# Pair sums one pair ahead, two buffers for their float32 weights, and GpSimd's last instruction

## Chip, core and metric

The kernel runs on one core of one Trainium2 chip. The metric is device time in microseconds (us) of one execution, as the median of several runs. Engines are called as the profile calls them: PE (TensorE matmul), PEld (its weight loads), DVE (VectorE), ACT (ScalarE), POOL (GpSimd), SP (SyncE, which only issues DMA transfers here, strictly in order).

## What is computed

Three stages in a row: causal attention mixed with a linear memory, and two gated feed-forward layers over the same 2304 tokens (4 sequences of 576, width 512 = 8 heads of 64, hidden width 1536).

```python
a = softmax(causal(q @ k.T / 8)); local = a @ v                       # per head, S = 576
mem = (phi(q) @ M_prev) / (phi(q) @ z_prev + 1e-6)                    # phi(x) = max(x, 0) + min(exp(x), 1)
x = sigmoid(beta) * mem + (1 - sigmoid(beta)) * local                 # -> 2304 x 512
xn = x / rms(x) * rms_g
x = (silu(xn @ w_gate) * (xn @ w_val)) @ w_out                        # layer 0
out = (sigmoid(x @ w2_gate) * (x @ w2_val)) @ w2_out                  # layer 1
```

## The kernel before

The tokens go through in five groups: first the first 128 tokens of all four sequences together (`g = -1`, 512 tokens, their attention written out by hand in the string `ORDER`), then the other 448 tokens of each sequence (`g = 0` to `3`). While PE does the two feed-forward layers of group g, the attention of group g+1 is traced in between, one step of the list `att_steps` after so many slices; `total` sets the pace (`len(steps) * (done - wait) // (total - wait)`). A scheduler then orders each engine's instructions, so program order is only partly the order of tracing.

A layer's hidden width is cut into 12 slices of 128 (`f`). A slice is two products with K = 512 (`pg`, gate, and `pv`, value, line 807), the nonlinearity on ACT and DVE (`gated`), and the slice's share of the layer's output (`out_share`, line 863, 12 matmuls into four accumulators `po`). Weights and tokens are split into two float16 or float32r parts, so each product is three matmuls.

In the last group (`last_slices`, `g = 3`) some slices go in pairs (`UNITS`: pairs 0-1 to 8-9 in layer 0, 3-4 to 9-10 in layer 1). `hidden_pair` computes a pair's 2 x 2 block product with seven products instead of eight (Winograd's form of Strassen's scheme; matmuls on line 959, results in `pw`). It needs sums of the two slices' weights: `weight_sums` loads the float32 weights of both slices (`kept`, two DMAs, line 912, tile `rw`), adds them on DVE (lines 919 and 927, tile `sw`), and splits the result into two float16 parts on ACT (929) and DVE (930). The products' partial sums are copied by ACT (`keep_sum`, 977) and added by DVE into `cw` (lines 980 and 1004). PE may write an accumulator again only after that DVE add has read it.

`rw` is the one buffer with tag "x" (before that, the attention's input). Of all pairs, only the first of layer 0 loads into spare weight slots. Weights themselves live in a ring of 13 slots (`ws`, `wl`, `wr`, `wrl`); a slot's load is issued by SP once its last reader is through.

POOL does four kinds of work. At the start it makes an identity and a causal mask (memsets, then AFFINE_SELECT, `masks.py:199` and line 92) from which ACT casts `ident_b` and `tri_b`, the operands of PE's first score matmuls (line 261). Up to 54 us it does some elementwise work of the first group (350, 343, 383). From then on it does only maxima over the partitions (PARTITION_ALL_REDUCE), the last of them for the scale of layer 1's tokens (`xtop`, line 1022). The built program has an instruction without operands, printed as ISA, ahead of POOL's first AFFINE_SELECT and another ahead of its first all-reduce.

After `xtop`, DVE multiplies the per-slice scales `unit[2]` of layer 1 by the new token scale (line 1167, ten slices at once).

```python
def unit_slices(f):
    nc.vector.tensor_scalar(
        out=unit[2][:, f], in0=unit[1][:, f], scalar1=st["half_is1"], scalar2=None, op0=ALU.mult
    )
```

Of the kernel before, what the change touches and what calls it, by code (L numbers as in the profile page):

```python
# [33 lines left out]
NWIDE = 2  # L34
# [26 lines left out]
def attn_moe_moe_kernel(ctx, tc, qT, kT, qk0, v, mz, beta, w8, rms_g, outT):  # L61
# [840 lines left out]
            nc.vector.tensor_scalar(out=q[:, 3], in0=q[:, 3], scalar1=half_isx, scalar2=None, op0=ALU.mult)  # L902
        return q

    def weight_sums(l, f, q, spare=False):

        raw = [slot(B - 1, F32) for i in range(2)] if spare else None
        if not spare:
            two = ap_.tile([128, 5, DM], F32, tag="x", name="rw")
            raw = [two[:, 2 * i:2 * i + 2] for i in range(2)]  # L910
        for i in range(2):
            nc.sync.dma_start(out=raw[i], in_=kept[l, f + i])
        out = []
        for m in range(2):
            part = lambda i, j: raw[i][:, m, 256 * j:256 * j + 256]
            ratio, less, scale = (q[:, c, (f - PAIRED[l]) // 2, m:m + 1] for c in (1, 2, 3))
            sw = ap_.tile([128, SW], F32, tag="sc", bufs=2, name="sw")[:, 0:1024]
            a = sw.rearrange("p (j n) -> j p n", j=4)
            nc.vector.tensor_tensor(out=a[0], in0=part(1, 0), in1=part(1, 1), op=ALU.add)
            for j, (x, c, y, op) in enumerate(  # L920
                (
                    (part(0, 0), less, a[0], ALU.add),
                    (part(0, 0), ratio, part(1, 0), ALU.subtract),
                    (part(0, 1), ratio, a[1], ALU.subtract),
                )
            ):
                nc.vector.scalar_tensor_tensor(out=a[j + 1], in0=x, scalar=c, in1=y, op0=ALU.mult, op1=op)  # L927
            w = slot(B - 1, F16).rearrange("p a b n -> p a (b n)")
            nc.scalar.activation(out=w[:, 0], in_=sw, func=AF.Copy, scale=scale)
            nc.vector.scalar_tensor_tensor(  # L930
                out=w[:, 1], in0=sw, scalar=scale, in1=w[:, 0], op0=ALU.mult, op1=ALU.subtract
            )
            out.append(w)
        return out

    def hidden_pair(ws, sums, l, f, xh, xs, hs, outs):

        n = NT
        regions = []
        for pool, tag in (("mm", "mm"), ("ps", "pa")):  # L940
            two = [late[pool].tile([128, 512], F32, tag=tag, name="pw") for _ in range(2)]
            regions.append([two[i // 2][:, 256 * (i % 2):256 * (i % 2) + n] for i in range(4)])

        def left(i, m, a, k):
            if i >= 3:
                return sums[m][:, a, 256 * (i - 3) + 128 * k:256 * (i - 3) + 128 * k + 128]
            c = 128 * k + (256 if i else 0)
            return ws[1 if i == 2 else 0][m][:, a, c:c + 128]

        def right(i, b, k):  # L950
            if i >= 3:
                return xs[b][:, i - 3, k]
            return xh[b][:, k + (2 if i else 0), n if i == 2 else 0:2 * n if i == 2 else n]

        def product(m, at, i, j, first=False):
            c = 0
            for k in range(2):
                for a, b in ((0, 0), (0, 1), (1, 0)):
                    nc.tensor.matmul(  # L959
                        regions[m][at],  # L960
                        left(i, m, a, k),
                        right(j, b, k),
                        start=first and c == 0,
                        stop=c == 5,
                        skip_group_check=True,
                    )
                    c += 1

        cs = []
        for m, tag in ((0, "kk"), (1, "qq")):  # L970
            cs.append([ap_.tile([128, S], F32, tag=tag, bufs=2, name="cw")[:, 0:2 * n] for _ in range(2)])
        one = [ap_.tile([128, S], F32, tag=t, bufs=1, name="sn") for t in ("kd", "qd")]
        three = [ap_.tile([128, 512], F32, tag=t, bufs=1, name="sn") for t in ("mx", "mb")]
        snaps = [[one[m][:, 0:n], one[m][:, n:2 * n], three[m][:, 0:n]] for m in range(2)]

        def keep_sum(m, i):
            nc.scalar.copy(out=snaps[m][i], in_=regions[m][0])

        def add(m, i, j, at, s):
            nc.vector.tensor_tensor(out=cs[m][i][:, j * n:(j + 1) * n], in0=regions[m][at], in1=snaps[m][s], op=ALU.add)  # L980

        R, Y, Q, V = range(4)
        A11, A12, A22, S1, S2, S3, S4 = range(7)
        B11, B21, B22, T1, T2, T3, T4 = range(7)
        for m in range(2):
            product(m, R, A11, B11, True)
            keep_sum(m, 0)
        for m in range(2):
            product(m, Q, A12, B21, True)
            add(m, 0, 0, Q, 0)  # L990
        for m in range(2):
            product(m, R, S2, T2)
            keep_sum(m, 1)
        for m in range(2):
            product(m, V, S1, T1)
        outs[0]()
        for m in range(2):
            product(m, R, S3, T3)
            keep_sum(m, 2)
            add(m, 1, 1, V, 2)  # L1000
        outs[1]()
        for m in range(2):
            product(m, Y, A22, T4)
            nc.vector.tensor_tensor(out=cs[m][1][:, 0:n], in0=snaps[m][2], in1=regions[m][Y], op=ALU.subtract)
        gated(cs[0][1], cs[1][1], l, f + 1, 2 * n, B - 1, hs[1])
        for m in range(2):
            product(m, V, S4, B22)
            add(m, 0, 1, V, 1)
        gated(cs[0][0], cs[1][0], l, f, 2 * n, B - 1, hs[0])
# [135 lines left out]
    def last_of(e):  # L1145
        return next(i for i in reversed(nc.cur_bb.bb.instructions) if i.engine == e)
# [14 lines left out]

    def first_sums(l):
        q = firsts["q", l] = pair_units(l)
        firsts[l] = weight_sums(l, PAIRED[l], q, l == 0)

    def unit_slices(f):
        nc.vector.tensor_scalar(
            out=unit[2][:, f], in0=unit[1][:, f], scalar1=st["half_is1"], scalar2=None, op0=ALU.mult
        )

    def last_slices(l, n, xt, halves, xs, po):
        g, f, pending, done = B - 1, 0, [], [0]
        ws, hs = {}, {}

        def share(i):
            out_share(ws[i], hs[i], po, n, done[0] == 0, done[0] == NF - 1)
            done[0] += 1

        for k, size in enumerate(UNITS[l]):
            for i in range(f, f + size):  # L1180
                ws[i] = weights(g, l, i)
                hs[i] = htiles(g, l, i)
            if l == 1 and f == NWIDE:
                unit_slices(slice(NWIDE, NF))
            if size == 2:
                sums = firsts[l] if f == PAIRED[l] else weight_sums(l, f, firsts["q", l])
                shares = [lambda: None] * (2 - len(pending)) + [lambda i=i: share(i) for i in pending]
                hidden_pair([ws[f], ws[f + 1]], sums, l, f, halves, xs, [hs[f], hs[f + 1]], shares)
                pending = [f + 1, f]
            else:  # L1190
                hidden(ws[f], l, f, n, g, halves if is_half(g, l, f) else xt, hs[f])
                for i in pending:
                    share(i)
                pending = [f]
            f += size
            if l == 0 and f == NF - 2:
                first_sums(1)
        for i in pending:
            share(i)

    for g in range(-1, B):
        n = 512 if g < 0 else S - 128
        steps = list(att_steps(g + 1)) if g + 1 < B else []

        total = 2 * NF - (8 if g <= 0 else 4 if g == 1 else 7)

        wait = 2 if g == 0 else 1
        if g == 0:
# [2 lines left out]
        for l in range(2):  # L1211
# [10 lines left out]
            for f in range(0 if g == B - 1 else NF + 1):  # L1222
                if f < NF:
                    if f >= early:
                        if g > 0 and l == 1 and f == NWIDE:
                            unit_slices(slice(NWIDE, NF))
                        turn = lagged(4 if g < 0 else 3) if g <= 0 else []
                        if g >= 0 and l == 0 and f in (1, 2):
                            turn = turn + tokens_done
                        with behind(turn):  # L1230
                            ws.append(weights(g, l, f))
                        hs.append(htiles(g, l, f))
                        if g == B - 2 and l == 1 and f == NF - 2:
                            first_sums(0)
                        hidden(ws[f], l, f, n, g, xh if l == 1 and is_half(g, l, f) else xt, hs[f])
                        marks.append(tuple(last_of(e) for e in (mybir.EngineType.Activation, mybir.EngineType.DVE)))
# [87 lines left out]
```

## Time and profile before

| what | before |
|---|---|
| time, median of 3 runs | 1061.79 us (1058.84 to 1062.64) |
| the profiled execution: its time, its span | 1061.79 us, 1060.0 us |
| PE busy | 1026.0 us (97% of the span), 6801 matmuls |
| DVE, ACT, POOL busy | 814.6, 591.8, 91.2 us |
[...]
| chain that ended last | PE 74%, DVE 11%, "issue" 6%, DMA 5%, ACT 3%, POOL 1% |

The span runs from the first to the last instruction of the execution; 1.8 us lie around it. "Issue" is time in which an engine waited for nothing that the profile shows. Busy time of PE is partly modelled, so only its gaps are read here, not its speed.

### The profile page before, as it was taken

What the parts mean: (1) busy time and instruction counts of PE and PEld (TensorE: products, weight loads), DVE (VectorE), ACT (ScalarE), POOL (GpSimd) and SP (SyncE); (2) the same over time, 40 slices, a digit from 0 to 9 for tenths busy, and PEclk for the clock granted to TensorE, in tenths of its full rate; (3) what the DMA queues carried; (4) which work ended last, traced back from release to release, by engine and by line L of the source; (5) the groups of instructions that cost most, each with busy time, mean ns of one, the idle gap of its engine ahead of it and who ended that gap; (6) DMA issues with size and microseconds to landing.
All of it is one profiled execution on the core that took longest, in us unless ns stands there. A gap on an engine that the chain in (4) does not pass through costs nothing.

```text
span 1060.0 us, 18472 instructions
## 1 busy us (share of the span) xinstructions
PE 1026.0 (97%) x6801; PEld 774.3 (73%) x6801; DVE 814.6 (77%) x1751; ACT 591.8 (56%) x1118; POOL 91.2 (9%) x84
## 2 busy tenths in 40 slices
PE   5899999999999999999999999999999999999998
PEld 3678887888766677776667867767677768987786
DVE  3978999988749989874677866648788778985772
ACT  3667878776758868762354543425446344442442
POOL 1401001010001202110010110001001000000000
PEclk9999999999999999999999999999999999999999
DMA  7299998975798466768654553675554348575440
GB/s 267 91 355 382 303 373 276 319 269 194 213 362 267 147 230 216 264 239 266 212 168 159 170 185 128 166 263 184 173 165 168 109 163 269 214 251 206 162 158 35
DMA packets 92283, 231.64 MB, mean 219 GB/s; under 512 B 24097, under 2 KB 30241, under 8 KB 92065
## 3 DMA queue, kind: packets, MB, share of 16 engines
q1 hardware_dynamic: 92192, 230.47, 64.0%
q8 instruction: 53, 0.87, 0.3%
q14 instruction: 38, 0.30, 0.1%
HBM read 182.72 MB, written 44.04 MB: 214 GB/s over the span
## 4 chain that ended last, share of the span: by engine, by line
PE 74%; DVE 11%; issue 6%; DMA 5%; ACT 3%; POOL 1%; SPq 0%; ACTq 0%; DVEq 0%; POOLq 0%
PE po L863 22%; PE pg L807 20%; PE pv L807 19%; PE ps L210 4%; PE pw L959 3%; DMA rw<-kept 3%; PE pm L580 1%; DVE sw L927 1%; PE pav L531 1%; PE pav L533 1%; PE pav L532 1%; DMA ha<-x 1%; PE po L860 1%; DMA kd<-in_kT 1%; DMA raw<-in_w 1%
## 5 line engine op out<-in xcount | busy, mean ns | idle before, releaser
L863 PE MATMUL po<-h,ws 128*128 128x448 f32 (+1 forms) x480 | 118.2, 385 | 0.0
L863 PE MATMUL po<-h,wl 128*128 128x448 f32 (+1 forms) x396 | 97.5, 386 | 0.0
L863 PEld LDWEIGHTS po<-h,ws 128*128 128x128 f32 x480 | 88.0, 188 | 11.7 <-ACT h L842 0.3
L515 POOL PARTITION_ALL_REDUCE mb<-mx x32 | 57.8, 1807 | 391.0 <-DVE mx L511 379.1
L807 PEld LDWEIGHTS <-ws 128*128 128x128 f16 x528 | 49.1, 98 | 49.0 <-issue 6.2
L863 PE MATMUL po<-h,wr 128*128 128x448 f32 x360 | 84.8, 378 | 0.0
L827 ACT ACTIVATE t<-pg,unit 128x448 f32<-128x448 f32 x70 | 44.2, 631 | 71.2 <-PE pg L807 71.2
L863 PEld LDWEIGHTS po<-h,wl 128*128 128x128 f32 x396 | 73.2, 188 | 9.4 <-ACT h L842 0.2
L807 PEld LDWEIGHTS <-wr 128*128 128x128 f16 x504 | 46.8, 98 | 43.7 <-issue 3.7
L475 ACT COPY sc<-ps 128x448 f32<-128x448 f32 (+5 forms) x128 | 52.3, 421 | 45.2 <-DVE sc L470 24.6
L842 ACT CAST h<-t 128x448 fp32r<-128x448 f32 (+1 forms) x70 | 40.6, 580 | 56.6 <-DVE t L831 51.2
L863 PEld LDWEIGHTS po<-h,wr 128*128 128x128 f32 x360 | 66.8, 188 | 6.3
L201 ACT ACTIVATE sc<-sc 128x1536 f32<-128x1536 f32 x32 | 47.5, 1485 | 35.8 <-DVE sc L524 29.9
L807 PEld LDWEIGHTS <-wl 128*128 128x128 f16 x408 | 38.1, 98 | 36.4 <-issue 5.0
L204 DVE TENSOR_TENSOR pt<-sc,pt 128x1536 f16<-128x1536 f32 x32 | 56.1, 1754 | 10.3 <-ACT pt L203 10.1
L210 PE MATMUL ps<-qq,kk 128*128 128x448 f32 (+2 forms) x160 | 57.4, 361 | 1.2 <-ACT sc L475 1.2
L843 DVE TENSOR_TENSOR h<-t,h 128x448 fp32r<-128x448 f32 (+1 forms) x70 | 45.5, 650 | 12.2 <-ACT h L842 11.8
L829 DVE SCALAR_TENSOR_TENSOR t<-t,pg 128x448 f32<-128x448 f32 (+2 forms) x50 | 31.0, 619 | 28.6 <-ACT t L827 28.6
L210 PE MATMUL ps<-q,kk 128*128 128x448 f32 (+2 forms) x160 | 49.4, 318 | 0.0
L837 DVE SCALAR_TENSOR_TENSOR t<-t,pv 128x448 f32<-128x448 f32 (+1 forms) x52 | 32.8, 631 | 19.3 <-PE pv L807 17.8
L203 ACT CAST pt<-sc 128x1536 f16<-128x1536 f32 x32 | 46.9, 1467 | 0.3
L531 PE MATMUL pav<-vh,pt 128*128 128x65 f16 x448 | 45.2, 195 | 0.5 <-ACT sc L475 0.5
(314 smaller groups left out, 2644.0 us busy)
## 6 DMA issues: line engine op xcount, KB each, us to landing
raw<-in_w SPq DMA_DIRECT2D x50, 511.8 KB, 6.3
ws<-parts SPq DMA_DIRECT2D x34, 512.0 KB, 4.1
wr<-parts SPq DMA_DIRECT2D x32, 512.0 KB, 4.0
kept<-w SPq DMA_DIRECT2D x48, 256.0 KB, 5.0
wl<-parts SPq DMA_DIRECT2D x23, 512.0 KB, 4.2
rawl<-in_w SPq DMA_DIRECT2D x22, 511.8 KB, 6.5
ws<-half SPq DMA_DIRECT2D x20, 512.0 KB, 3.8
wr<-half SPq DMA_DIRECT2D x20, 512.0 KB, 3.7
```

The costliest lines, as they stand in the source:

```text
L201: nc.scalar.activation(out=sc[:, 0:n], in_=sc[:, 0:n], func=AF.Exp, scale=scale)
L203: nc.scalar.copy(out=pt[:, 0, 0:n], in_=sc[:, 0:n])
L204: nc.vector.tensor_tensor(out=pt[:, 1, 0:n], in0=sc[:, 0:n], in1=pt[:, 0, 0:n], op=ALU.subtract)
L210: nc.tensor.matmul(ps[:, c0:c0 + n], kk[:, k0:k0 + 128], r[:, q0:q0 + n], start=(i == 0), stop=(i == 1 and not mask))
L475: nc.scalar.copy(out=sc[:, d:d + n], in_=ps[:, c:c + n])
L515: nc.gpsimd.partition_all_reduce(mb[:, 0:448], mx[:, 0:448], channels=128, reduce_op=bass_isa.ReduceOp.max)
L531: nc.tensor.matmul(ps, ph, vh1[:, vt, h, :], start=first, stop=False)
L807: nc.tensor.matmul(ps[:, 0:n], w[:, a, k * 128:(k + 1) * 128], x[b][:, k, o:o + n], start=(i == 0), stop=(i == 3 * KD - 1))
L827: nc.scalar.activation(out=t, in_=pg[:, 0:n], func=AF.Tanh, scale=u[:, 0:1] if half else 0.5)
L842: nc.scalar.copy(out=hi, in_=t)
L843: nc.vector.tensor_tensor(out=lo, in0=t, in1=hi.bitcast(F32), op=ALU.subtract)
L863: nc.tensor.matmul(po[d][:, 0:n], w[2][:, a, c], hh[:, b, 0:n], start=(first and i == 0), stop=(last and i == 2))
```

## The change

Three parts.

1. `weight_sums` is split. `pair_load` issues the two DMAs of a pair's float32 weights, ahead of the `hidden_pair` of the pair before; the sums themselves are traced inside that `hidden_pair`, by `sums_next`, after the product V and queued on DVE behind the second `add` of the products Q (`first_row`).
2. The float32 weights alternate between two buffers: `rw` as before, and `rd`, which takes the tag "d" (otherwise the low part of layer 1's tokens, `xd`).
3. In the last group `unit_slices` gives slices 2 to 7 to DVE and 8 to 11 to POOL, as one TENSOR_SCALAR. It is then POOL's last instruction.

Besides, the attention of the last group is paced one share tighter (`total` smaller by one) and the first pair's sums of layer 0 are traced one slice earlier.

```diff
-    def weight_sums(l, f, q, spare=False):
-
-        raw = [slot(B - 1, F32) for i in range(2)] if spare else None
-        if not spare:
-            two = ap_.tile([128, 5, DM], F32, tag="x", name="rw")
+    def pair_load(l, f):
+
+        k = (f - PAIRED[l]) // 2
+        if l == 0 and k == 0:
+            raw = [slot(B - 1, F32) for i in range(2)]
+        else:
+            if (k + l) % 2:
+                two = ap_.tile([128, 5, DM], F32, tag="x", name="rw")
+            else:
+                two = xp.tile([128, KD, NMAX], F32, tag="d", name="rd")
             raw = [two[:, 2 * i:2 * i + 2] for i in range(2)]
         for i in range(2):
             nc.sync.dma_start(out=raw[i], in_=kept[l, f + i])
+        return raw
+
+    def weight_sums(l, f, q, raw):
+
         out = []
...
         for m in range(2):
             product(m, Q, A12, B21, True)
             add(m, 0, 0, Q, 0)
+        first_row = last_of(mybir.EngineType.DVE)
         for m in range(2):
             product(m, R, S2, T2)
             keep_sum(m, 1)
         for m in range(2):
             product(m, V, S1, T1)
+        with tc.issue_after(first_row):
+            sums_next()
         outs[0]()
...
-        firsts[l] = weight_sums(l, PAIRED[l], q, l == 0)
-
-    def unit_slices(f):
-        nc.vector.tensor_scalar(
-            out=unit[2][:, f], in0=unit[1][:, f], scalar1=st["half_is1"], scalar2=None, op0=ALU.mult
-        )
+        firsts[l] = weight_sums(l, PAIRED[l], q, pair_load(l, PAIRED[l]))
+
+    def unit_slices(g):
+        mid = NF if g < B - 1 else NF // 2 + 2
+        for e, c in ((nc.vector, slice(NWIDE, mid)), (nc.gpsimd, slice(mid, NF))):
+            if c.start < c.stop:
+                e.tensor_scalar(out=unit[2][:, c], in0=unit[1][:, c], scalar1=st["half_is1"], scalar2=None, op0=ALU.mult)
...
-                sums = firsts[l] if f == PAIRED[l] else weight_sums(l, f, firsts["q", l])
...
+                if k + 1 < len(UNITS[l]) and UNITS[l][k + 1] == 2:
+                    raw = pair_load(l, f + 2)
+
+                    def sums_next():
+                        firsts[l, f + 2] = weight_sums(l, f + 2, firsts["q", l], raw)
+                else:
+                    sums_next = lambda: None
+                sums = firsts[l] if f == PAIRED[l] else firsts[l, f]
...
-        total = 2 * NF - (8 if g <= 0 else 4 if g == 1 else 7)
+        total = 2 * NF - (8 if g <= 0 else 4 if g == 1 else 8)
...
-                        if g == B - 2 and l == 1 and f == NF - 2:
+                        if g == B - 2 and l == 1 and f == NF - 3:
                             first_sums(0)
```

Three places in the built programs follow. **POOL, the end of its program, before.** `xtop` is the maximum for layer 1's scale.

```order
L1022 ISA xtop<-am_9418 128x1
L515 ISA mb<-mx 128x448 x4
L1022 ISA xtop<-am_11359 128x1
L1320 UNCONDITIONAL_BRANCH
L1320 ISA
```

The same place in the changed program:

```order
L1034 ISA xtop<-am_9489 128x1
L515 ISA mb<-mx 128x448 x3
L1034 ISA xtop<-am_11359 128x1
L1182 ISA
L1182 TENSOR_SCALAR unit_124<-unit_123,inv 128x8
L1340 UNCONDITIONAL_BRANCH
```

Behind the last all-reduce stand an ISA without operands, as at the other changes of kind, and the elementwise multiply.

**DVE, layer 1 of the last group, at the end of pair 3-4, before.** `pw_11549` to `pw_11552` are the accumulators of this pair, `rw_11864` holds the weights of slices 7 and 8.

```order
L980 TENSOR_TENSOR cw_11554<-pw_11550,sn_11559 128x224
L980 TENSOR_TENSOR cw_11556<-pw_11552,sn_11560 128x224
L1004 TENSOR_TENSOR cw_11554<-sn_11559,pw_11549 128x224
L1004 TENSOR_TENSOR cw_11556<-sn_11560,pw_11551 128x224
L919 TENSOR_TENSOR sw_11867<-rw_11864 128x256
L927 SCALAR_TENSOR_TENSOR sw_11867<-rw_11864,pu_11197 128x256
L919 TENSOR_TENSOR sw_11875<-rw_11864 128x256
L927 SCALAR_TENSOR_TENSOR sw_11875<-rw_11864,pu_11197 128x256
L980 TENSOR_TENSOR cw_11553<-pw_11550,sn_11557 128x224
```

The same place in the changed program, where `pw_11553` to `pw_11556` are the pair's accumulators, `pw_11717` one of the next pair's, and `rw_11711` the weights of slices 7 and 8:

```order
L989 TENSOR_TENSOR cw_11560<-pw_11556,sn_11564 128x224
L989 TENSOR_TENSOR cw_11558<-pw_11554,sn_11563 128x224
L1016 TENSOR_TENSOR cw_11560<-sn_11564,pw_11555 128x224
L1016 TENSOR_TENSOR cw_11558<-sn_11563,pw_11553 128x224
L989 TENSOR_TENSOR cw_11559<-pw_11556,sn_11562 128x224
L989 TENSOR_TENSOR cw_11557<-pw_11554,sn_11561 128x224
L837 SCALAR_TENSOR_TENSOR t_11548<-t_11548,cw_11560 128x448
L837 SCALAR_TENSOR_TENSOR t_11542<-t_11542,cw_11559 128x448
L989 TENSOR_TENSOR cw_11720<-pw_11717,sn_11723 128x224
L928 TENSOR_TENSOR sw_11780<-rw_11711 128x256
```

Before, four sums of the pair 7-8 stood ahead of the last two adds of the pair 3-4; now all six adds of the pair 3-4 stand ahead of them, and an add of the next pair too.

**SP, layer 1 of the last group, before.** `half` is the float16 gate and value weight of a slice, `parts` its output weight, `kept` its float32 weights; the number behind `_1_` is the slice.

```order
L773 DMA ws_11490<-parts_1_2_2_2445 128x1024
L762 DMA wl_11543<-half_1_4_5409 128x2048
L912 DMA rw_11864<-kept_1_7_2950 128x1024
L762 DMA ws_11852<-half_1_7_5628 128x2048
L912 DMA rw_11864<-kept_1_8_3023 128x1024
L773 DMA ws_11854<-parts_1_7_2_2972 128x1024
```

And after:

```order
L917 DMA rd_11550<-kept_1_5_2804 128x1024
L773 DMA ws_11490<-parts_1_2_2_2445 128x1024
L917 DMA rd_11550<-kept_1_6_2877 128x1024
L762 DMA wrl_11705<-half_1_6_5560 128x2048
L773 DMA ws_11707<-parts_1_6_2_2899 128x1024
L762 DMA wl_11544<-half_1_4_5409 128x2048
L917 DMA rd_11884<-kept_1_9_3096 128x1024
L762 DMA wr_11699<-half_1_5_5492 128x2048
L917 DMA rd_11884<-kept_1_10_3169 128x1024
```

The weights of slices 7 and 8 are now asked for long before this place (ahead of the layer's first weights), and slice 5's weight `half_1_5`, which stood well ahead of it, stands behind the float32 load of slice 9, which may only be issued when the sums of 5 and 6 have read `rd`.

## Rows read from the trace of the kernel before

**Rows 1.** POOL in order of time: start, length, line, operation, idle before and its end.

```profile
14.02 0.28 POOL masks.py:199 TENSOR_SCALAR_AFFINE_SELECT ident<-ident 128x128 f32<-128x128 f32 x1 [12.48 <-issue]
...
15.98 1.54 POOL L350 TENSOR_SCALAR e<-e 128x512 f32<-128x512 f32 x1 [0.96 <-ACT e L346]
...
53.69 0.55 POOL L383 TENSOR_TENSOR ri<-ss,half_neg 128x1 f32<-128x1 f32 x1 [1.02 <-DVE ss L380]
...
973.67 0.36 POOL L1022 PARTITION_ALL_REDUCE xtop<-am  x1 [124.44 <-DVE am L1020]
```

**Rows 2.** PE in order of time, the first two rows.

```profile
1.23 4.02 PE L125 MATMUL pw<-warm 128*128 128x512 bf16 x9 [1.23 <-DVE warm L122]
...
15.41 1.03 PE L261 MATMUL ps<-ident_b,tri_b 128*128 128x512 bf16 x2 [10.15 <-ACT tri_b L102]
```

**Rows 3.** Busy time of each engine (us, instructions) by stretch, clock, DMA.

```profile
15.40:65.00 49.60, 44.55 (x336) 35.89 (x336) 43.64 (x117) 35.05 (x111) 15.76 (x12) 1.00 0.52 176
...
90.00:880.00 790.00, 782.93 (x5132) 573.62 (x5131) 625.56 (x1343) 466.87 (x844) 73.08 (x61) 1.00 0.67 222
...
880.00:1054.80 174.80, 169.76 (x1227) 145.74 (x1225) 126.69 (x258) 73.37 (x136) 0.36 (x1) 1.00 0.52 186
```

**Rows 4.** SP's DMA issues in order of time, at the start.

```profile
0.73 0.39 SPq L224 DMA_DIRECT2D qk<-in_qk  x1
...
3.14 0.53 SPq L117 DMA_DIRECT2D mzt<-in_mz  x1
3.71 0.44 SPq L118 DMA_DIRECT2D g_bc<-in_rms_g  x1
```

**Rows 5.** The same transfers: count, KB, us from issue to landing.

```profile
qk<-in_qk SPq DMA_DIRECT2D x1, 512.0 KB, 3.5
...
mzt<-in_mz SPq DMA_DIRECT2D x1, 1040.0 KB, 11.1
g_bc<-in_rms_g SPq DMA_DIRECT2D x1, 256.0 KB, 11.6
```

**Rows 6.** The first readers of `g_bc` (DVE) and `mzt` (PE), in order of time.

```profile
22.70 0.68 DVE L674 TENSOR_REDUCE gm<-g_bc 128x1 f32<-128x512 f32 x1
...
25.40 0.61 PE L360 MATMUL pm<-mzt,e 128*128 128x130 f32 x4
```

**Rows 7.** Waits of PE, 880 to 1060 us: us in total, times, longest.

```profile
PE pw L959 <- DVE cw L980: 2.6, 3, 1.8
PE pw L959 <- DVE cw L1004: 1.4, 2, 1.0
PE pw L959 <- ACT sn L977: 0.8, 3, 0.3
```

**Rows 8.** PE in order of time in the last group.

```profile
937.77 1.31 PE L959 MATMUL pw<-ha,wr 128*128 128x224 f16 x12 [0.96 <-DVE cw L1004]
...
990.05 1.23 PE L959 MATMUL pw<-hb,wl 128*128 128x224 f16 x11
...
1000.43 1.31 PE L959 MATMUL pw<-hb,wr 128*128 128x224 f16 x12
1003.50 0.73 PE L959 MATMUL pw<-hb,wr 128*128 128x224 f16 x6 [1.76 <-DVE cw L980]
...
1017.81 1.31 PE L959 MATMUL pw<-hb,ws 128*128 128x224 f16 x12 [0.48 <-DVE cw L1004]
```

**Rows 9.** DVE groups, 880 to 1055 us: count, busy us, mean ns, idle before.

```profile
L927 DVE SCALAR_TENSOR_TENSOR sw<-rw,pu,sw 128x256 f32<-128x256 f32 x32 | 15.0, 477 | 0.0
L927 DVE SCALAR_TENSOR_TENSOR sw<-rw,pu 128x256 f32<-128x256 f32 x16 | 7.7, 478 | 0.0
...
L919 DVE TENSOR_TENSOR sw<-rw 128x256 f32<-128x256 f32 x16 | 6.7, 420 | 7.6 <-DMA rw<-kept 7.6
```

**Rows 10.** DMA issues, 900 to 1030 us: count, KB, median us to landing.

```profile
rw<-kept SPq DMA_DIRECT2D x12, 512.0 KB, 4.9
...
wr<-half SPq DMA_DIRECT2D x6, 512.0 KB, 3.7
```

More of the change, by code (lines that the diff above doesn't have):

```diff
@@ L934, in weight_sums, with hidden_pair @@
         return out
-    def hidden_pair(ws, sums, l, f, xh, xs, hs, outs):
+    def hidden_pair(ws, sums, l, f, xh, xs, hs, outs, sums_next):
         n = NT
@@ L1183, in last_slices @@
             if l == 1 and f == NWIDE:
-                unit_slices(slice(NWIDE, NF))
+                unit_slices(g)
             if size == 2:
-                sums = firsts[l] if f == PAIRED[l] else weight_sums(l, f, firsts["q", l])
                 shares = [lambda: None] * (2 - len(pending)) + [lambda i=i: share(i) for i in pending]
-                hidden_pair([ws[f], ws[f + 1]], sums, l, f, halves, xs, [hs[f], hs[f + 1]], shares)
+                if k + 1 < len(UNITS[l]) and UNITS[l][k + 1] == 2:
[5 more added lines that the diff above has]
+                sums = firsts[l] if f == PAIRED[l] else firsts[l, f]
+                hidden_pair([ws[f], ws[f + 1]], sums, l, f, halves, xs, [hs[f], hs[f + 1]], shares, sums_next)
                 pending = [f + 1, f]
@@ L1225, in attn_moe_moe_kernel @@
                         if g > 0 and l == 1 and f == NWIDE:
-                            unit_slices(slice(NWIDE, NF))
+                            unit_slices(g)
                         turn = lagged(4 if g < 0 else 3) if g <= 0 else []
```

## The prediction

> **What bounds the kernel now.** I read the windows first. From 90 to 880 us PE is busy 782.93 of 790.00 us, and from 880 us to the last matmul 169.76 of 174.80 us, at a granted clock of 1.00 throughout [rows 3]. What other engines save there is worth only what PE waits for: 7.1 us in the first stretch, 5.0 us in the second. The instruction count of PE is the same after the change (the edits add no matmul), so a gain can come from two places only: those 5.0 us, and the time before PE is loaded.
>
> The second view is the order of time at the start. PE does its warm-up matmuls, then nothing for 10.15 us, until ACT has cast `tri_b` [rows 2]. ACT waits for POOL's mask, and POOL waits for nothing that the profile names: ahead of the first AFFINE_SELECT at 14.02 us lie 12.48 us put down to "issue" [rows 1]. The reader should see that PE, ACT and POOL all stand behind this one gap, and that nothing else in the execution leaves PE idle for so long.
>
> The third view is the list of waits of PE in the last group: 4.8 us in all, nearly all of it for DVE adds (lines 980 and 1004) that empty an accumulator, and ACT's copies behind them [rows 7]. The fourth says why those adds come late. DVE works in order, and a sum of the next pair's weights stood ahead of them and waited for its float32 weights: 7.6 us of DVE's idle time ended with the DMA into `rw` [rows 9]. The largest PE gap, 1.76 us at 1003.50 us, is of this kind [rows 8]; the order before the change shows the four sums ahead of the add it waited for.
>
> **Part 1 and 2: sums one pair earlier, two buffers.** Removed is the wait for `rw`. With one buffer a load could be asked for only when the sums of the pair before had read it, 4.9 us before it lands [rows 10]; with two, the weights of slices 7 and 8 stand in SP's order ahead of the layer's first weights. The gaps that stand behind such a wait are 0.96, 1.76 and 0.48 us [rows 8], with two smaller ones of the same adds and of ACT behind them 4.8 us together [rows 7]. Some of the 4.8 us are short hand-overs that no order removes, so I take 3.6 us off: the three named gaps (3.2 us) and half of what is left over from ACT (0.4 of 0.8 us). Bounds: 0, if the adds are late for another reason, and 4.8.
>
> Added is a wait on SP. Slice 5's weight `half_1_5` now stands behind the float32 load of slice 9, which waits until the sums of 5 and 6 have read `rd`. Those sums may begin when the first row of the pair 3-4 is through, four of fourteen products, so about a quarter of the pair's 10.4 us (990.05 to 1000.43 us [rows 8]): 992.6 us. They read `rd` in two instructions of 0.42 and six of 0.48 us (16 and 32 + 16 over the eight pairs of this stretch [rows 9]), 0.84 + 2.88 = 3.7 us, with an add or two in between 4.4 us: 997.0 us. SP then issues two transfers, and 3.7 us later (the median of `half` [rows 10]) slice 5's weight is there: 1000.9 us, against a pair that begins at 1000.43 us. I price it at 0.7 us; bounds 0, and 2.9 us with the landing time of a later, fuller queue (4.9 us instead of 3.7, and DVE 1 us behind). Queued behind it are only loads for the pairs after, with over 10 us in hand. At the other pairs two shares of output (about 5 us of PE work) lie between, and the same wait is covered; without that cover each would cost the same 0.7 us.
>
> The extra load into `rd` in layer 0 goes out while PE does group 2 and DMA is half idle; its price is nothing, and at most one landing, 4.9 us, if `xd` were read later than I think. The sums' own instructions are the same in number. Tighter pacing of the attention moves work within 90 to 880 us, where PE has 7.1 us of gaps in 790 [rows 3]; I take 0, bounds -1 and +1.
>
> **Part 3: an elementwise instruction at POOL's end.** The multiply itself (128 x 8) is small, and its first reader is the nonlinearity of slice 8, at the end of pair 7-8, after 1017.81 us [rows 8]. [...] What counts is the state it leaves. The order shows an ISA without operands wherever POOL changes from all-reduces to elementwise work or back; the only "issue" gap of this size stands behind the first of them. After it, elementwise instructions follow one another from 15.98 to 53.69 us, and each gap ends with a named engine [rows 1]. So the 12.48 us are paid for a change of kind, not for an instruction. Before the change, POOL ends each execution with an all-reduce [rows 1], so the next one begins with a change of kind. [...]
>
> [...]
>
> How far can the start then move? PE's warm-up ends at 1.23 + 4.02 = 5.25 us [rows 2]; the first `qk` has landed at 0.73 + 3.5 = 4.2 us [rows 4, 5]; the mask, 12.4 us earlier, would be cast by about 3 us. So the first scores could begin 10.16 us earlier. What is late next is `g_bc`: it lands at 3.71 + 11.6 = 15.3 us, and DVE reads it at 22.70 us [rows 4 to 6], so from there on DVE can be at most 7.4 us ahead. `mzt` (14.2 us, read at 25.40) allows 11.2. From 15.40 to 65.00 us DVE is busy 43.64 of 49.60 us [rows 3] and the chain runs through it, so little of the lost 2.8 us comes back: I take 7.4 us.  PE, full from 65 us on, hands those 7.4 us through to the end.
>
> **Sum.** 1061.8 (the profiled execution, equal to the median shown) - 7.4 (start) - 3.6 (PE gaps) + 0.7 (SP) = 1051.5 us.
>
> **Rivals.**
> [...]
> [...]
> - *Slower: weights queued behind float32 loads.* SP issues in order, and now float32 loads that wait for sums stand ahead of weights of the coming pair. If DVE does its sums 2 us later than I work out (it has 126.69 us of work in 174.80 [rows 3]), the slice's weight is late at every pair boundary, not only at 5-6: 2 us beyond the hand-over at seven boundaries is 14 us. With the start unmoved and no gap saved that is 1075.8 us. It makes the kernel slower as a whole from 0.8 us at each boundary (5.5 us in all) if nothing else is gained, and from 2.1 us against all that I count. For it: DVE is the fuller engine beside PE here; against it: two output shares cover most boundaries.
> - *The sums part does nothing* and only the start counts: 1061.8 - 7.4 = 1054.4 us.
>
> **Chances.** Forecast (start moved, gaps saved): 0.53. The fourth rival (start alone): 0.07, 1054.4 us, faster. Part of the gap: 0.07, faster. Fetched again: 0.25; with the most that the gaps could give (4.8 us, 0.45%) it stays within 0.5%, but for 0.02. Slower: 0.08. So faster by over 0.5%, about what a measurement of this kernel can tell from no change (5.3 us): 0.69; within it 0.23; slower 0.08. The range: downwards the start at its bound of 10.15 and the gaps at 4.8 give 1046.8 us; upwards it takes in the first rival, 1058.9. That leaves out the slower case and the ends of the others: 1046.5 to 1059.5. The forecast's own range is 1046.8 to 1055.6 (start 5, gaps 1.9, SP 0.7).
>
> **What would show it.** Start: the "issue" gap ahead of AFFINE_SELECT shrinks from 12.48 us to under 3, the first row of PE at line 261 comes at about 5.3 us, and DVE waits for `g_bc` up to 2.8 us. If that gap is still 12 us, step 3 is wrong, whatever the time. Gaps: DVE no longer waits for `rw` or `rd`, and PE's waits after 870 us on `cw` fall from 4.0 us to under 1. SP: PE waits at the first product of pair 5-6 for the DMA into a weight slot, under 1.5 us. What would make the forecast wrong: state lost between executions, a later binder of the start than `g_bc` (a raw weight, `qk` of the third sequence), or weights late at several pairs.

## The result, and the profile after

The changed kernel took 1051.61 us (median of 5 runs, 1050.36 to 1054.33) against 1061.79 us before (5 runs, 1058.84 to 1063.50): a ratio of 0.9908, 95% interval 0.9885 to 0.9931. It is faster by about 10 us. Its profiled execution took 1051.61 us, with a span of 1049.5 us, 10.5 us less than the span before. The forecast was 1051.5 us. Its sum had three terms, and the trace shows that the total is nearer than the terms are.

POOL in order of time, at the start and at the end of the changed kernel (start, length, engine, line, operation, idle before):

```profile
1.00 0.53 POOL L712 MEMSET top<- 128x512 int32 x1
1.82 0.29 POOL masks.py:199 TENSOR_SCALAR_AFFINE_SELECT ident<-ident 128x128 f32<-128x128 f32 x1 [0.29 <-POOL top L712]
...
967.88 0.36 POOL L1034 PARTITION_ALL_REDUCE xtop<-am  x1 [124.57 <-DVE am L1032]
975.59 0.86 POOL L1182 TENSOR_SCALAR unit<-unit,inv 128x8 f32<-128x8 f32 x1 [7.35 <-ACT h L846]
```

The 12.48 us of "issue" ahead of the first AFFINE_SELECT [rows 1] are 0.29 us now. PE and DVE at the start:

```profile
4.95 0.59 PE L261 MATMUL ps<-ident_b,tri_b 128*128 128x512 bf16 x2
...
16.00 1.97 PE L312 MATMUL ps<-v,qk 128*128 128x64 f32 x8 [3.18 <-DVE pw L657]
```

```profile
10.28 0.69 DVE L278 TENSOR_REDUCE m<-ps 128x4 f32<-128x512 f32 x1
14.59 0.69 DVE L674 TENSOR_REDUCE gm<-g_bc 128x1 f32<-128x512 f32 x1 [3.62 <-DMA g_bc<-in_rms_g]
```

The scores begin 10.46 us earlier than in [rows 2]. Then DVE's reduction of `g_bc`, 8.11 us earlier than in [rows 6], waits 3.62 us for its transfer, and PE stands 3.18 us behind DVE. PE's granted clock is lower when it goes on. Below is the busy time by stretch, in the order of the columns of [rows 3]; third from the right is the granted clock:

```profile
15.00:20.00 5.00, 4.00 (x17) 3.65 (x18) 3.41 (x18) 2.02 (x9) 0.00 (x0) 0.51 1.04 409
20.00:25.00 5.00, 4.84 (x37) 3.74 (x36) 3.51 (x8) 1.89 (x3) 1.24 (x1) 0.81 0.25 96
```

The granted clock is 0.51 in the first stretch and 0.81 in the second, and 1.00 from 10 to 15 and from 25 to 45 us. Eight matmuls on line 312 take 1.97 us at 16.00 us, and 1.08 us at 11.53. The same view of the profile before prints 1.00 for both stretches, as [rows 3] do from 15.40 us on. PE's own rows there say otherwise. Two matmuls on line 261 take 1.03 us at 15.41 us [rows 2], and the next two as long:

```profile
18.39 1.04 PE L261 MATMUL ps<-ident_b,tri_b 128*128 128x512 bf16 x2
```

In the changed kernel they take 0.59 us at 4.95 us. The profile before holds no record of the clock ahead of 20.6 us, and the view counts time without a record as full speed. So I take it that the kernel before, too, ran at a lower clock when PE went on after its gap of 10.15 us. The profiles of experiments 2, 10 and 11, which have the gap of 12 to 13 us on POOL as well, print 0.50 from 10 to 15 us and 0.50, 0.60 and 0.61 from 15 to 20 us.

PE's waits in the last group, 860 to 1050 us (total, times, longest), and the rows where it waited longest and where the prediction looked:

```profile
PE pw L968 <- DMA wr<-half: 1.4, 1, 1.4
PE pw L968 <- DVE cw L989: 0.9, 2, 0.5
PE pw L968 <- DMA wl<-half: 0.3, 1, 0.3
PE pw L968 <- DVE tc L888: 0.3, 1, 0.3
PE pg L807 <- ACT t L827: 0.3, 1, 0.3
```

```profile
898.44 1.32 PE L968 MATMUL pw<-tc,wr 128*128 128x224 f16 x12 [1.42 <-DMA wr<-half]
...
994.27 2.47 PE L968 MATMUL pw<-hb,wr 128*128 128x224 f16 x24
```

The waits of [rows 7] for `cw` and `sn` fell from 4.8 to 0.9 us, and the pairs of layer 1 wait for nothing that the view shows. DVE no longer waits for `rw` or `rd`. A wait of 1.4 us for a weight has come, in layer 0.

To place the 10.5 us I use three marks that stand in every profile: the first output products that read a `ws` buffer (line 863, 12 matmuls of 128x512), the last all-reduce into `xtop`, and the last 12 output products. In the changed kernel:

```profile
89.62 2.96 PE L863 MATMUL po<-h,ws 128*128 128x512 f32 x12
...
1042.75 2.59 PE L863 MATMUL po<-h,ws 128*128 128x448 f32 x12
```

Before, they stand at 94.98, 973.67 and 1052.22 us; after, at 89.62, 967.88 and 1042.75. The start gave 5.36 us, the 878 us between the first two marks 0.43, layer 1 of the last group (last two marks) 78.55 - 74.87 = 3.68, and the end behind them 1.03 (7.78 against 6.75 us to the end of the span): 10.5 us in all.

### The profile page after: what moved, and what is told of

It is laid out like the page before. It is cut to its first block, busy times and chain, and to the rows that moved or that the text cites. A ratio compares the mean times of both kernels' runs of the same rounds, so it can differ in the third digit from the quotient of the medians.

```text
span 1049.5 us, 18469 instructions
## 1 busy us (share of the span) xinstructions
PE 1025.9 (98%) x6797; PEld 776.0 (74%) x6801; DVE 814.8 (78%) x1751; ACT 590.0 (56%) x1118; POOL 91.3 (9%) x85
## 4 chain that ended last, share of the span: by engine, by line
PE 76%; DVE 8%; issue 4%; ACT 4%; DMA 3%; POOL 0%; SPq 0%; ACTq 0%; DVEq 0%; POOLq 0%
PE po L863 23%; PE pg L807 20%; PE pv L807 19%; PE pw L968 5%; PE ps L210 4%; PE pm L580 1%; PE pav L531 1%; PE pav L533 1%; PE pav L532 1%; DMA ha<-x 1%; DMA wr<-half 1%; PE po L860 1%; DVE sw L936 1%; DMA wl<-half 0%; DMA kd<-in_kT 0%
## 5 line engine op out<-in xcount | busy, mean ns | idle before, releaser
L863 PE MATMUL po<-h,ws 128*128 128x448 f32 (+1 forms) x504 | 123.5, 385 | 0.0
L863 PEld LDWEIGHTS po<-h,ws 128*128 128x128 f32 x504 | 92.5, 188 | 11.8 <-DVE h L843 0.3
L863 PE MATMUL po<-h,wl 128*128 128x448 f32 (+1 forms) x384 | 94.8, 386 | 0.0
L827 ACT ACTIVATE t<-pg,unit 128x448 f32<-128x448 f32 x70 | 44.2, 631 | 74.9 <-PE pg L807 74.8
L807 PEld LDWEIGHTS <-wr 128*128 128x128 f16 x528 | 49.1, 98 | 46.5 <-issue 4.6
L863 PE MATMUL po<-h,wr 128*128 128x448 f32 x348 | 81.3, 377 | 0.0
L863 PEld LDWEIGHTS po<-h,wl 128*128 128x128 f32 x384 | 70.9, 188 | 9.2 <-ACT h L842 0.2
L863 PEld LDWEIGHTS po<-h,wr 128*128 128x128 f32 x348 | 64.5, 188 | 5.7
L807 PEld LDWEIGHTS <-wl 128*128 128x128 f16 x384 | 35.8, 98 | 33.9 <-issue 4.5
L837 DVE SCALAR_TENSOR_TENSOR t<-t,pv 128x448 f32<-128x448 f32 (+1 forms) x52 | 32.8, 632 | 20.6 <-PE pv L807 19.1
```

The lines of the kernel that those rows point to most:

```text
L807: nc.tensor.matmul(ps[:, 0:n], w[:, a, k * 128:(k + 1) * 128], x[b][:, k, o:o + n], start=(i == 0), stop=(i == 3 * KD - 1))
L827: nc.scalar.activation(out=t, in_=pg[:, 0:n], func=AF.Tanh, scale=u[:, 0:1] if half else 0.5)
L863: nc.tensor.matmul(po[d][:, 0:n], w[2][:, a, c], hh[:, b, 0:n], start=(first and i == 0), stop=(last and i == 2))
```

## The experiments

The kernel before ran beside experiments 1 to 4, 5 to 8 and 9 to 12 on the same chip, with medians of 1060.37, 1061.18 and 1060.83 us, so kernels of different groups are compared by their ratio to it.

**1. Part 3 alone.** The kernel before, with only the split of the unit multiply:

```
+    def unit_slices(g):
+        mid = NF if g < B - 1 else NF // 2 + 2
+        for e, c in ((nc.vector, slice(NWIDE, mid)), (nc.gpsimd, slice(mid, NF))):
...
```

> The kernel before with part 3 alone (POOL multiplies the units of slices 12 to 19 in the last group; sums and buffers as before). [...] Rival: the start moved because other instructions stand elsewhere with all three parts; then the gap stays at 12.5 us and the time at 1061.8 us.

Measured: 1053.59 us, ratio 0.9937 (0.9919 to 0.9955). The gap ahead of AFFINE_SELECT is 0.29 us, and the first mark stands at 88.61 us, 6.4 us earlier than before. DVE waits 3.2 us for `g_bc` here too. The rival falls: the start needs none of the other edits. I had expected a gap under 1 us and about 1056.5 us, ratio 0.995; the size is above that, 6.8 us instead of 5.3, with 0.995 just inside the interval. (POOL multiplies slices 8 to 11 here, as in the changed kernel, not 12 to 19.)

**2. The sums part alone.** The changed kernel with DVE multiplying all units:

```
-        mid = NF if g < B - 1 else NF // 2 + 2
+        mid = NF
```

> The changed kernel without part 3 (DVE multiplies all units of the last group, so POOL ends with an all-reduce). My theory: the issue gap at the start is back at 12.5 us and the first output share at 66.9 us; the last group keeps what it gained, 3.6 us in layer 1 and up to 1.5 us around it: 1056.5 to 1058 us. Rival 1, sums do nothing: 1061.8 us. Rival 2, the gain of the last group came with the shorter tail that part 3 leaves: about 1060.5 us.

Measured: 1056.30 us, ratio 0.9958 (0.9945 to 0.9972). POOL at the start:

```profile
14.98 0.28 POOL masks.py:199 TENSOR_SCALAR_AFFINE_SELECT ident<-ident 128x128 f32<-128x128 f32 x1 [13.45 <-issue]
```

The gap is back, the first mark is at 96.10 us, and layer 1 of the last group takes 74.79 us, close to the 74.87 us of the changed kernel. Both rivals fall, and the time is just below the range that I gave. Alone the two halves give 6.8 and 4.1 us; together they give 8.8 to 10.2 us (changed kernel, fifth experiment and first result), so they add up within their intervals. The sums part holds the two buffers, the new place of the sums, the tighter pacing and the earlier first sums. Experiments 6 and 7 take the first two apart; the other two were not run alone.

**3. `g_bc` read later.** The changed kernel with the reduction held behind DVE's last instruction of the first tokens' pipeline:

```
-                token_scale()
+                with tc.issue_after(z["lo"]):
+                    token_scale()
```

> The changed kernel with the reduction of g_bc placed behind DVE's last instruction of the first tokens' pipeline, so that nothing reads g_bc before some 40 us. My theory: the start gave 5.3 instead of 7.4 us because DVE waited 3.62 us for g_bc, PE ran out of work and its granted clock fell to about half for a stretch. Without that wait the granted clock stays near 1.00 from 10 to 25 us, the first output share comes at 58 to 59.5 us instead of 61.55, and the time is 1048 to 1050 us. Rival 1, the next transfer (mzt, or v) binds at nearly the same time: DVE or PE waits there instead, the time stays within 1 us of 1051.6. Rival 2, the clock would fall anyway: granted clock 0.5 again somewhere between 10 and 25 us, at most 1 us gained.

Measured: 1048.86 us, ratio 0.9888 (0.9869 to 0.9906). The reduction starts at 42.5 us and waits for nothing. Busy time by stretch:

```profile
10.00:15.00 5.00, 4.18 (x29) 2.99 (x28) 4.04 (x13) 5.00 (x27) 0.63 (x1) 1.00 1.01 416
15.00:20.00 5.00, 4.74 (x42) 3.85 (x42) 4.46 (x12) 3.08 (x8) 1.87 (x2) 1.00 1.03 411
20.00:25.00 5.00, 4.08 (x30) 3.16 (x30) 4.83 (x13) 3.79 (x16) 3.12 (x3) 1.00 0.76 265
```

```profile
85.00 2.95 PE L863 MATMUL po<-h,ws 128*128 128x512 f32 x12
```

The clock stays at 1.00, with the same transfers running. The first mark is 9.98 us ahead of before: nearly all of PE's gap of 10.15 us [rows 2] arrives, and neither `mzt` nor `v` binds next: a weight load of PE waits 0.4 us for `mzt`, nothing waits for `v`. So the wait for `g_bc`, with what came behind it, cost the changed kernel 4.62 us of its start. Only part of that is left at the end. From the first mark to the last all-reduce this profile takes 879.28 us against 878.26.

**4. An all-reduce behind the multiply.** The changed kernel, with one more instruction on POOL:

```
+        if g == B - 1:
+            end = ap_.tile([128, 2], F32, tag="wtop", bufs=3, name="wtop")
+            nc.gpsimd.partition_all_reduce(end, unit[2][:, NF - 1], channels=128, reduce_op=bass_isa.ReduceOp.max)
```

> The changed kernel with one more all-reduce on POOL behind the multiply, over units that the multiply wrote, into a tile that nobody reads. My theory: the kind of the last instruction is what counts, so the issue gap ahead of the first AFFINE_SELECT is back at 12.5 us, the first output share at 66.9 us, and the time 1051.6 + 5.3 = 1057 us. Rival: an elementwise instruction anywhere behind the reductions is enough, or the multiply's leaving DVE is what helps: gap under 1 us and 1051.6 us.

Measured: 1057.67 us, ratio 0.9969 (0.9954 to 0.9984), near the second experiment. POOL at its start and end:

```profile
14.27 0.28 POOL masks.py:199 TENSOR_SCALAR_AFFINE_SELECT ident<-ident 128x128 f32<-128x128 f32 x1 [12.74 <-issue]
...
974.71 0.36 POOL L1034 PARTITION_ALL_REDUCE xtop<-am  x1 [124.01 <-DVE am L1032]
982.01 0.73 POOL L1182 TENSOR_SCALAR unit<-unit,inv 128x8 f32<-128x8 f32 x1 [6.94 <-DVE t L837]
989.72 0.37 POOL L1185 PARTITION_ALL_REDUCE wtop<-unit  x1 [6.98 <-issue]
```

The multiply is there, POOL still does it, and the start is as slow as before: only the kind of POOL's last instruction has changed. The last row is worth reading twice. A change of kind inside the execution shows as 6.98 us of "issue", which nobody waits for here. The 6.94 us ahead of the multiply are put down to a DVE instruction whose result it does not read: its scale `inv` was there 6.6 us before it began.

**5. The changed kernel again**, beside the next three.

> The changed kernel once more, beside the others of this call: ratio 0.990 to 0.992 by every theory. Its start is what I look at: my theory says that DVE waits for g_bc here too and that the granted clock falls between 13 and 25 us.

Measured: 1052.40 us, ratio 0.9923 (0.9904 to 0.9943), a little above the range expected, with the earlier 0.9908 inside its interval. DVE waits 4.71 us for `g_bc` (PE also waits for `qk`, 1.7 us, and for `v`, 0.7 us), the clock is 0.79 from 15 to 20 us and 0.87 from 20 to 25, and the first mark is at 88.86 us.

**6. One buffer.** Every float32 load after the first goes into `rw`:

```
-            if (k + l) % 2:
-                two = ap_.tile([128, 5, DM], F32, tag="x", name="rw")
-            else:
-                two = xp.tile([128, KD, NMAX], F32, tag="d", name="rd")
+            two = ap_.tile([128, 5, DM], F32, tag="x", name="rw")
```

> The changed kernel with one buffer (every float32 load but the first goes to rw, as before), sums traced inside the pair before, part 3 kept. Theory A, the place of the sums does it: the load has most of a pair (over 8 us) between the sums that free rw and the sums that read it, no wait of DVE for rw, PE's waits after 860 us at 3 to 4 us, time within 1.5 us of the changed kernel. Theory B, as my prediction had it, the second buffer removes the wait: DVE waits for rw again, 5 us or more in all, and PE's waits are back at about 5 us or more, with weights late behind the float32 loads: 1.5 to 4 us slower than the changed kernel.

Measured: 1051.78 us, ratio 0.9914 (0.9893 to 0.9936). DVE has no wait for `rw`, and PE's waits after 860 us are 2.6 us, fewer than the 3 to 4 us that I expected. Theory A: with the sums inside the pair before, one buffer is enough.

**7. Two buffers, sums in their old place.**

```
-        with tc.issue_after(first_row):
-            sums_next()
...
-                sums = firsts[l] if f == PAIRED[l] else firsts[l, f]
+                sums = firsts[l] if f == PAIRED[l] else weight_sums(l, f, firsts["q", l], raws[f])
```

> The changed kernel with the loads in two buffers, asked for a pair ahead, but the sums traced ahead of their own pair, as before; part 3 kept. Theory A, the place of the sums does it: DVE has no wait for the load, but the four sums (3.7 us or more of DVE) still stand ahead of the first adds of the pair; PE waits for those adds 3 us or more in all, and the time is 1.5 to 4 us above the changed kernel. Theory B, the wait for the load was the whole trouble: PE's waits are as small as in the changed kernel (about 3 us) and the time is within 1 us of it.

Measured: 1052.74 us, ratio 0.9923 (0.9902 to 0.9943), equal to the changed kernel beside it. PE's waits after 860 us:

```profile
PE pw L968 <- DVE tc L888: 1.2, 1, 1.2
PE pw L968 <- ACT sn L986: 0.4, 2, 0.2
PE pg L807 <- ACT t L827: 0.3, 1, 0.3
PE po L863 <- ACT h L842: 0.3, 1, 0.3
PE pw L968 <- ACT tc L887: 0.2, 1, 0.2
```

DVE waits 2.6 us for the two buffers together, where it waited 7.6 us [rows 9], and PE does not wait for a single `cw` add. Here theory B holds for PE: the instructions of the sums alone hold up no add. With the sixth experiment this says that either edit is enough. The new place of the sums alone ends DVE's wait for the load; the second buffer alone cuts it to 2.6 us.

**8. Loads kept in the order of the program, on the third experiment's kernel.**

```
-        for i in range(2):
-            nc.sync.dma_start(out=raw[i], in_=kept[l, f + i])
+        with tc.issue_after(last_of(mybir.EngineType.SP)):
+            for i in range(2):
+                nc.sync.dma_start(out=raw[i], in_=kept[l, f + i])
```

> The third experiment's kernel (g_bc read later), and every pair's float32 load kept behind the weight loads traced ahead of it in SP's order. My theory: the 1.0 to 1.4 us of PE for slice 3's weights at the third product row of pair 2-3 come from half_0_3 standing behind a float32 load that waits for rw; with that order it is issued earlier, that wait goes, and the time is 1 us below the third experiment's (ratio about 0.988 against 0.9888). Rival: half_0_3 waits for its own slot, so the wait stays as it is and only the float32 loads come later, no gain, or up to 3 us of DVE waits for rw and rd come back.

Measured: 1049.62 us, ratio 0.9892 (0.9870 to 0.9914). PE's waits after 860 us:

```profile
PE pw L969 <- DVE t L829: 1.0, 1, 1.0
PE pw L969 <- DVE cw L990: 0.8, 2, 0.5
PE pw L969 <- ACT sn L987: 0.6, 1, 0.6
PE pw L969 <- DMA wl<-half: 0.5, 1, 0.5
PE pw L969 <- DVE tc L888: 0.4, 1, 0.4
```

The wait for `wr` is gone, so the order on SP made it. My gain did not come: the waits sum to 3.6 us with the row for line 807 (0.3 us), against 2.3 us in the third experiment, and layer 1 takes 75.45 us instead of 74.75. DVE waits for `rd` again, 1.0 us, as the rival had it.

**9. The kernel before, profiled again.**

> The kernel before, profiled once more. Open is why its layer 1 of the last group (from the last all-reduce to the last matmuls) took 78.55 us in the profile shown, and 76.6 us with part 3 alone, whose sums are the same: if a load's landing decides it, a second profile shows another length (76 to 78.5 us) and another wait of DVE for rw (6 to 8 us); if part 3 does it, 78.5 us again. The same for the tail behind DVE's last instruction, 4.67 us there and 3.6 us in every other kernel.

Measured: 1061.79 us, span 1059.7 us. Its waits of PE after 860 us and its last marks:

```profile
PE pw L959 <- ACT sn L977: 2.0, 4, 1.2
PE pw L959 <- DVE cw L1004: 1.5, 1, 1.5
PE pw L959 <- DVE cw L980: 1.0, 1, 1.0
```

```profile
975.12 0.36 POOL L1022 PARTITION_ALL_REDUCE xtop<-am  x1 [125.28 <-DVE am L1020]
...
1051.95 2.59 PE L863 MATMUL po<-h,ws 128*128 128x448 f32 x12
```

Layer 1 takes 76.83 us, and DVE waits 6.6 us for `rw`. In layer 1 the longest wait for `cw` is 1.0 us; the 1.8 us of [rows 7] belong to one execution. The end behind DVE's last instruction is 4.65 us long, as in the profile shown (4.67). In both, the last output transfer takes 3.3 us from issue to landing.

**10. `g_bc` read later in the kernel before** (the edit of the third experiment).

> The kernel before with the reduction of g_bc placed later, as in the third experiment. My theory: without the earlier start nothing waits for g_bc, so the edit alone is worth nothing: 1060 to 1062.5 us, ratio 0.998 to 1.002. Rival: the reduction's place in DVE's row order is worth something by itself (DVE is the fullest engine until 65 us): 1 to 3 us faster.

Measured: 1062.01 us, ratio 1.0010 (0.9993 to 1.0027). The edit is worth nothing by itself, only behind the earlier start.

**11. A memset as POOL's last instruction, in the kernel before.**

```
+                end = ap_.tile([128, 2], F32, tag="wtop", bufs=3, name="wtop")
+                with tc.issue_after(last_of(mybir.EngineType.Pool)):
+                    nc.gpsimd.memset(end, 0)
```

> The kernel before with a memset of 128 x 2 elements on POOL behind the last all-reduce. [...] Rival: any instruction of POOL's own after the all-reduces leaves the right state: gap under 1 us, about 1055 us.

Measured: 1060.84 us, ratio 1.0001 (0.9988 to 1.0015). I had expected the gap to stay at 12.5 us and the time at 1061 us. POOL at both ends:

```profile
13.65 0.28 POOL masks.py:199 TENSOR_SCALAR_AFFINE_SELECT ident<-ident 128x128 f32<-128x128 f32 x1 [12.11 <-issue]
...
973.89 0.36 POOL L1022 PARTITION_ALL_REDUCE xtop<-am  x1 [124.03 <-DVE am L1020]
974.12 0.17 POOL L1187 MEMSET wtop<- 128x2 f32 x1
```

The memset follows the all-reduce at once, where the multiply of the fourth experiment came 6.94 us behind it, and it leaves the start as it was, with a gap of 12.11 us. The rival falls: a memset is not of the kind that matters.

**12. One buffer and `g_bc` later together.**

> The changed kernel with one buffer and with the reduction of g_bc placed later. If the two are independent, as both single experiments have it: ratio 0.987 to 0.9895, 1047 to 1050 us, first share of the first full layer at 85 us. If the earlier start puts more load on the queue of float32 loads, DVE waits for rw again and the ratio is above 0.990.

Measured: 1050.53 us, ratio 0.9907 (0.9893 to 0.9921), above the range for independent edits. The first mark is at 86.22 us. DVE does not wait for `rw`, so the reason that I gave for such a ratio is wrong too: PE waits 3.4 us for `wr` and `wl` weights after 860 us, against 1.0 us in the third experiment, and from the first mark to the last all-reduce it takes 880.61 us. What of this is one buffer's doing stays open.

## Why the prediction was right, and where its terms were not

**The start: cause right, size wrong.** With the multiply last (eight profiles) the gap is 0.29 us. With an all-reduce last it is 12.0 to 13.5 us, in kernels with the sums part (experiments 2 and 4) and without it (before, 9, 10), and a memset last leaves it at 12.1. Experiment 4 differs from the changed kernel only at the end of its program, and so the execution before is what can bring that to the start of the next. So it is shown from both sides that POOL's last instruction decides on the gap. That something of POOL's state stays from one execution to the next was an assumption of mine in the forecast. What it is that stays no run shows: in the profile before no packet of the two queues that the page calls "instruction" moved from 1.6 to 14 us, and no run is of a first execution or of two programs in turn. "Fetched again" in the chances, with 0.25, is a start that stays as it is: with the gaps saved that is 1061.8 - 3.6 + 0.7 = 1058.9 us, which the range takes in upwards. No run shows that anything is fetched; the runs show a gap of 0.29 us or of 12.0 to 13.5. An unmoved start falls by experiment 1 alone. So does "part of the gap", 0.07, a gap of about half of the 12.48 us. The fourth rival, sums that do nothing, falls by the 4.1 us of experiment 2.

The change of kind inside the execution shows as 6.98 us (experiment 4), the gap at the start as 12.0 to 13.5 us. No run here tells why that one is longer.

The term of the sum was 7.4 us and measured 5.36. Over more profiles it is 4.7 to 6.7: the first mark stands at 94.6 to 96.0 us (mean 95.3) in before, 9, 10 and 11, and at 88.6 to 90.7 (mean 89.6) in the changed kernel and experiments 1, 5, 6 and 7. The binder was named rightly: `g_bc`. DVE waited 3.62 us for it, more than the 2.8 that I allowed, yet its reduction came 8.11 us earlier (in experiments 1, 5, 6 and 7 it came at 15.1 to 15.9 us, 6.8 to 7.6 us earlier), so the limit of 7.4 us was about right. The step that failed is the one behind it: that what DVE is ahead there reaches PE, and the end, whole. POOL's first operation on line 343, before and after:

```profile
29.69 1.64 POOL L343 TENSOR_TENSOR x<-x,av 128x512 f32<-128x512 f32 x1 [2.86 <-DVE x L562]
```

```profile
23.77 1.65 POOL L343 TENSOR_TENSOR x<-x,av 128x512 f32<-128x512 f32 x1 [9.05 <-DVE x L562]
```

Of the 8.11 us, 5.92 are left there: from DVE's reduction to this row it took 6.99 us before (6.7 to 7.2 in the four others with the gap and the early read) and 9.18 after, and in between DVE waited 2.7 us for PE, which had stood empty for 3.18 us and then ran at a granted clock of 0.51 (15 to 20 us) and 0.81 (20 to 25 us). My sum had no term for this. In the other profiles the loss is smaller where the clock is higher. The two stretches average 0.83 in experiment 1 (0.70 and 0.96) and in experiment 5 (0.79 and 0.87), and 0.66 in the changed kernel. The first marks of the two stand at 88.61 and 88.86 us, against 89.62, though in experiment 5 the reduction came 1.32 us later than in the changed kernel (15.91 against 14.59 us). How the loss is shared between the clock and the empty PE was not measured apart. Without the wait (experiment 3) the bound that I gave for the start, 10.15 us, was nearly reached, with 9.98 us.

**The gaps: near in size, but laid in part to the wrong layer.** I took 3.6 us. PE's waits for `cw` and `sn` in the last group fell by 3.9 us. But 0.96 us of my three gaps lie in layer 0 (937.77 us [rows 8]), where a wait for a weight has come instead, and layer 1 alone lost 3.68 us. Its waits for `cw` and `sn` were 2.9 us of that, and none are left; the rest stands in no wait of the view. This is also large for the kernel: layer 1 of the kernel before took 76.55 to 76.93 us in four other profiles with the sums as before (1, 9, 10, 11), against 78.55 us in the one that I read; with the sums part, or the half of it that 6 and 7 keep, it took 74.7 to 74.9 us in seven, and 75.5 and 75.7 in experiments 8 and 12. The usual gain is about 2 us. The largest gap of [rows 8], 1.76 us, which was half of my term, is one landing of one execution: in the other four, PE's waits for `cw` in layer 1 are 0.6 to 1.1 us in all.

**SP: right kind, wrong place.** I priced 0.7 us for slice 5 of layer 1, behind a float32 load that waits for `rd`. PE does not wait there (994.27 us). It waited 1.42 us for slice 3 of layer 0, behind the load of slice 6 into `rw`, and experiment 8, which changes the order on SP, took that wait away. I had called the same wait covered at the other pairs by two output shares, 24 matmuls. Here four of them ran between SP's issue at 890.71 us and the wait, and the transfer took 7.7 us from its issue, where I had reckoned with the 3.7 us of [rows 10]. A slip in that sum did not matter: four of fourteen products are 3.0 us of the pair's 10.4, not 2.6.

**What the sum left out.** The end behind the last products is 1.03 us shorter. It varies: from DVE's last instruction to the end of the span it took 3.6 to 5.3 us in five profiles with the old sums, and 3.6 to 3.7 us in every profile with the new ones. What varies is the landing of the last output transfers: they took up to 3.3 us before (4.1 in experiment 11) and up to 2.3 after. Why is open.

So the nearness of 1051.5 us is luck: 2.0 us too much at the start stood against 1.03 us at the end, which the sum did not hold, and 1.21 us more than 3.6 - 0.7 between the first mark and the last one (0.43 + 3.68). Over the other profiles, the change is worth 5.7 us at the start (mean of five against mean of four first marks), about 2 us in layer 1, and some 1 us of varying end. The rival on weights queued at every boundary, which would have made the kernel slower, came true at one pair only, for 1.4 us.

**A version faster than both.** Reading `g_bc` later gave ratios of 0.9888 and 0.9892 in experiments 3 and 8, against 0.9908 and 0.9923 for the changed kernel. The intervals overlap, so 2 to 4 us are likely rather than measured. Experiment 12, with the same edit, lies at 0.9907. In these three kernels (3, 8, 12) the stretch from the first mark to the last all-reduce takes 879.3 to 881.1 us, where it takes 876.8 to 878.4 in the five that start early and wait for `g_bc`. So part of what the start gains is given back before the last group's layer 1, and why is open.

## What to carry to other kernels

When an engine's first instruction stands behind a gap that waits for nothing, ask what the last instruction of the same program leaves behind: an execution is followed by the next one of its kind. When a start is moved up, every transfer that was early enough becomes a candidate for the next wait, and the work behind a wait can pay for more than the wait: here a PE that stood empty for 3.18 us and a granted clock of 0.51 came behind it. A clock of 1.00 in a view should be checked against the length of equal matmuls (here 1.03 against 0.59 us). A gap of 1 or 2 us behind a transfer should be read in a second profile before it becomes a term, and two edits that remove the same wait count once.

## What the runs showed of the hardware

- The end of POOL's program decides on the gap ahead of its first AFFINE_SELECT when the program runs again: 0.29 us where the last instruction is an elementwise multiply, 12.0 to 13.5 us where it is an all-reduce, or a memset behind one.
- The change of kind late in the execution shows as 6.94 and 6.98 us in experiment 4, with DMA at a share of 0.27 and 0.75 in those stretches, and as 12.74 us at the start of the same execution, with DMA at 0.90. Ahead of the multiply the eight profiles in which it is last show 6.9 to 8.7 us.
- After 10.15 us without matmuls (before) PE's first two matmuls of 512 columns on line 261 take 1.03 us and the next two 1.04, against 0.59 us at a granted clock of 1.00 (changed kernel, 4.95 us). Experiments 2, 10 and 11, with 13.45, 12.37 and 12.11 us ahead of the first AFFINE_SELECT, print a granted clock of 0.50 from 10 to 15 us and of 0.50 to 0.61 from 15 to 20 us.
